# Attention and two MLPs on one NeuronCore: another order of issue, and block 0 transposed in full rows

## The chip, the core and the metric

The kernel runs on one NeuronCore of a Trainium2 chip. The engines are TensorE (PE; its weight loads are listed apart as PEld), VectorE (DVE), ScalarE (ACT), GpSimd (POOL) and SyncE (SP), which issues the DMAs. The metric is device time in microseconds, the median of the runs of one kernel.

## The reference, cut to what matters

```python
# x: (2, 4096, 192), weight_gen: (2, 4096, 8, 7); 8192 tokens in all
w = softmax(weight_gen, axis=-1)                     # 7 taps for each of 8 heads
x_pad = 6 zero rows ahead of each batch's x
attn[b, s, h, :] = sum_k w[b, s, h, k] * x_pad[b, s + k, h, :]     # 24 columns a head
h1 = attn.reshape(8192, 192) @ w1_in                 # 192 -> 2048
z  = (h1 * sigmoid(h1)) @ w1_out                     # 2048 -> 192
h2 = z @ w2_in                                       # 192 -> 2048
P  = a[0] + a[1]*h2 + a[2]*h2**2 + a[3]*h2**3
Q  = 1 + |b[0]|*|h2| + |b[1]|*h2**2
out = (P / (Q + 1e-6)) @ w2_out                      # 2048 -> 192
```

All is fp32. For PE each fp32 operand is split into a high part, rounded to PE's fp32r format, and a low part, the rest (g1h and g1l, g2h and g2l, xh and xl, and the weights wa, wb, wo), and products of the parts are summed.

## The kernel before, in words

The 8192 tokens are cut into 16 blocks of 512, numbered 0 to 15. For a block the kernel makes the attention (products of x with the softmax weights, 4 and 3 taps at a time, and their sums), transposes it, and runs it through both MLPs. Each MLP is cut into 8 units of 256 of its 2048 columns, and a unit's tile is 128 x 1024.

Since the 192 columns are 128 + 64, PE is used as two halves of 64 rows each, which work at the same time ("64*128" in the rows); a matmul of one half has 512 columns. What both write lies in one PSUM bank pair, and one half writes one side of it while the other half writes the other. Then the sides change, and to keep them apart a `nop` on SP (line 388) waits for both halves and releases both.

Work is given out in operations with a short name, a dot and the block, such as `l2.5`. The ones used below:

- `M`, `m`: products for 4 and 3 taps (line 728, POOL or DVE); `p`, `r`, `a`: their sums (lines 738, 742 and 748)
- `Z.0`, `X`: load the rows of x (line 690); `W0`, `W1`: 84 and 16 transposes whose results aren't used, at the start (lines 766 and 761)
- `T`, `TR`: the block's transposes in halves of 64 rows, one side and then the other (line 799); `XH`, `XL`: the split of the result into xh and xl
- `A`, `K`: a unit's first-layer matmuls into the bank h, one side and then the other (10 and 8; `B`, `Q` in the second MLP); `S`, `H`, `L`: silu, g1h and g1l (ACT, ACT, and DVE line 901)
- `C`, `E`, `I`, `F`: a unit's second-layer matmuls into acc0 (6, 4, 6, 4; `D`, `P`, `J`, `R` into acc1)
- `U`, `V`, `u`, `w`, `Y`, `N`, `G`, `g`: the rational function of the second MLP; on DVE `u` (line 948) and `w` (line 951) read h in PSUM and t in SBUF, `Y` (line 957) and `g` (line 968) read SBUF alone
- `h`, `l`: g2h (POOL line 453, ACT line 451 or DVE line 455) and g2l (line 978, DVE or POOL), both from SBUF

The order is written out by hand in `ORDER` (lines 39 to 266), a list of 3957 entries. In `name@n:s` the number n chooses the engine from those that the operation allows, and s the buffer or bank that it gets. A `^` in front of it loads an activation table. `Plan.run` (line 304) issues the entries one after the other. PE operations go to `Lanes`, which keeps a queue and a clock for each half and always issues for the half that is behind. A `|` in front of a PE entry is a bar: it moves the clock of the lagging half on by one turn (as long as one matmul of 512 columns), so that this half gets less work then. Other operations wait in the list `later` until the PE work that they need is issued. The planner costs nothing at run time; the list alone sets each engine's order.

Of the kernel before, what the change touches and what calls it, by code (L numbers as in the profile page):

```python
# [20 lines left out]
P = 128  # L21
J = 64
JB = 4
NB = J // JB
BT = JB * P
D = 192
DL = D - P
# [22 lines left out]
    q0O340:D q0O341 q0O3h@1 q0O3x L4.0:h q1B0a1 q1B0a0 cr q1B040:B q1B041 X.2 AW.2 |A6.0:A F5.0 K6.0 C5.0 E2.0 E1.0  # L50
    E3.0 S6.0 H6.0:r q1A0a0 A7.0:D L6.0:d q1B0h1 q1B0x1 q1A040:A q1B0h0 q1B0x0 a3.1 I3.0 F3.0 I4.0 K7.0 E6.0 E5.0
    C3.0 E4.0 C4.0 C6.0 T.1:B S7.0 q1A0a1 q1A041 H7.0:s q1O0l0:c q1O1l1:l q1O1l0:i L7.0:n ||||I6.0 TR.1 F7.0 I5.0
    F6.0 F4.0 I7.0 q1A1l0:m q1O0a1 q1O0a0 q1A0h q1O040:D q1O041 q1A1l1:r q1A0x q1O0h q1O2l0:c XH0.1:q q1O0x XL0.1:y
    m1.2:g M1.2:k M3.2:v m2.2:o p1.2@1 m0.2:w M2.2:p M0.2:t r1.2@1 m3.2:x p3.2@1 p2.2@1 r2.2@1 p0.2@1 r0.2@1 r3.2@1
# [10 lines left out]
    P2.0 u4.0 w4.0 U6.0:x ^^N3.0 h0.0@1:a T.2:C D1.0 TR.2 h5.0:v Y4.0 r0.3 u6.0 l5.0@1:r E6.1 C7.1 J0.0 J2.0 J1.0
    R1.0 XH0.2:m G3.0 XL0.2:n EC.1:f V6.0:y EM.1 g3.0 R5.0 A0.2:C Y6.0 N4.0 G4.0 N6.0 w6.0 EA.1 XH1.1:k G6.0 h3.0:p
    l3.0:o a0.3@1:e a2.3 XL1.1:s l0.0:u g6.0 g4.0 D0.0 K0.2 R2.0 B7.0:A D3.0 P5.0 Q7.0 B1.1:B J5.0 J3.0 ^S0.2 V7.0:q
    H0.2:a Q1.1 h6.0:h L0.2:r Y7.0 U7.0:g D5.0 P3.0 D6.0 P0.0 l6.0@1:v A3.2:C V1.1:p ^^N7.0 G7.0 U1.1:l u7.0 w7.0
    h4.0@2:x g7.0 R0.0 J6.0 B2.1:A R6.0 K3.2 J4.0 Q2.1 s3e l4.0@1:y h7.0:b l7.0@1:j M1.3:t u1.1 w1.1 s3t ^S3.2
# [343 lines left out]
def kernel(  # L413
# [13 lines left out]
    pe, act, dve, pool, sp = nc.tensor, nc.scalar, nc.vector, nc.gpsimd, nc.sync  # L427
# [249 lines left out]
    def attention(b):  # L677
# [96 lines left out]
        if b == 0:  # L774
            plan.op("W1", b, "PE", warm_h, rd=[at[0], ("ident", 0), (*tp, 0)], wr=[("h", 0, 0, 0, 0)])
# [339 lines left out]
```

## Time and profile before

| | us |
|---|---|
| median of 3 runs | 1260.79 |
| the runs | 1259.11, 1260.79, 1264.77 |
| the profiled execution's own time | 1258.52 |
| its span in the profile | 1256.7 |
| PE busy | 1193.0 (95%) |
| PE weight loads busy | 1020.4 (81%) |
| DVE busy | 1143.7 (91%) |
| ACT busy | 1041.0 (83%) |
| POOL busy | 509.4 (41%) |

Busy time is a mean over two stages, the first 100 us, in which data and weights come in, and the steady part after it. A busy PE is not PE at its peak, since matmuls overlap. The chain of waits is the sequence of work followed back from the last instruction, at each step to what released it.

### The profile page before, as it was taken

What the parts mean: (1) busy time and instruction counts of PE and PEld (TensorE: products, weight loads), DVE (VectorE), ACT (ScalarE), POOL (GpSimd) and SP (SyncE); (2) the same over time, 40 slices, a digit from 0 to 9 for tenths busy, and PEclk for the clock granted to TensorE, in tenths of its full rate; (3) what the DMA queues carried; (4) which work ended last, traced back from release to release, by engine and by line L of the source; (5) the groups of instructions that cost most, each with busy time, mean ns of one, the idle gap of its engine ahead of it and who ended that gap; (6) DMA issues with size and microseconds to landing.
All of it is one profiled execution on the core that took longest, in us unless ns stands there. A gap on an engine that the chain in (4) does not pass through costs nothing.

```text
span 1256.7 us, 24901 instructions
## 1 busy us (share of the span) xinstructions
PE 1193.0 (95%) x10340; PEld 1020.4 (81%) x10340; DVE 1143.7 (91%) x1037; ACT 1041.0 (83%) x1012; POOL 509.4 (41%) x326
## 2 busy tenths in 40 slices
PE   4989999999999999999999999999999999999997
PEld 4757778788788877899887888778888999789885
DVE  7989999899989888899999898998988989998997
ACT  4769988897898987798887788879897888789786
POOL 5874464345436333445214554332423313340332
PEclk9989999999999999999999999999999999999999
DMA  8650010102020010100100020010100001000001
GB/s 210 190 161 21 10 51 14 44 2 58 5 68 1 16 61 1 46 9 26 48 1 26 33 75 1 1 57 1 54 1 5 18 1 57 1 23 1 10 1 38
DMA packets 17753, 45.42 MB, mean 36 GB/s; under 512 B 2412, under 2 KB 9194, under 8 KB 17640
## 3 DMA queue, kind: packets, MB, share of 16 engines
q1 hardware_dynamic: 17640, 43.83, 11.6%
q8 instruction: 81, 1.33, 0.4%
q14 instruction: 32, 0.26, 0.1%
HBM read 31.73 MB, written 7.90 MB: 32 GB/s over the span
## 4 chain that ended last, share of the span: by engine, by line
PE 62%; DVE 19%; ACT 10%; issue 5%; SPq 2%; POOL 1%; DMA 1%; DVEq 0%; ACTq 0%; POOLq 0%
PE acc L786 31%; PE h L786 29%; DVE y L957 3%; DVE t L968 3%; DVE t L948 3%; DVE t L951 2%; DVE g1l L901 2%; ACT y L942 2%; ACT t L938 1%; DVE pr L728 1%; ACT y L962 1%; ACT h L893 1%; ACT g1h L897 1%; ACT y L965 1%; DVE dec L602 1%
## 5 line engine op out<-in xcount | busy, mean ns | idle before, releaser
L786 PE MATMUL h<-xh,wa 64*128 64x512 f32 x2048 | 464.6, 397 | 23.1 <-DVE t L951 9.1
L786 PEld LDWEIGHTS h<-xh,wa 64*128 64x128 f32 x2048 | 284.2, 185 | 76.5 <-SPq L388 17.2
L786 PE MATMUL h<-xl,wa 64*128 64x512 f32 x1024 | 312.8, 390 | 0.1
L786 PE MATMUL h<-xh,wb 64*128 64x512 f32 x1024 | 311.5, 389 | 0.0
L786 PE MATMUL acc<-g1h,wo 64*128 64x512 f32 x1536 | 299.0, 393 | 0.5 <-DVE t L951 0.4
L786 PE MATMUL acc<-g2h,wo 64*128 64x512 f32 x1536 | 292.6, 392 | 3.7 <-SPq L388 3.2
L978 POOL TENSOR_TENSOR g2l<-t,g2h 128x1024 fp32r<-128x1024 f32 x66 | 169.3, 2567 | 219.3 <-ACT g2h L451 62.5
L786 PEld LDWEIGHTS acc<-g2h,wo 64*128 64x128 f32 x1536 | 208.6, 184 | 27.5 <-SPq L388 6.9
L786 PEld LDWEIGHTS acc<-g1h,wo 64*128 64x128 f32 x1536 | 208.9, 185 | 24.5 <-SPq L388 3.8
L786 PE MATMUL acc<-g2l,wo 64*128 64x512 f32 x1024 | 213.7, 393 | 6.0 <-DVE g2l L978 4.1
L786 PE MATMUL acc<-g1l,wo 64*128 64x512 f32 x1024 | 212.4, 397 | 3.1 <-DVE g1l L901 2.6
L968 DVE SCALAR_TENSOR_TENSOR t<-t,a_sb,y 128x1024 f32<-128x1024 f32 x128 | 185.4, 1455 | 5.0 <-ACT y L965 4.0
L957 DVE SCALAR_TENSOR_TENSOR y<-y,b_sb 128x1024 f32<-128x1024 f32 x128 | 184.1, 1447 | 5.7 <-ACT y L942 5.4
L901 DVE TENSOR_TENSOR g1l<-h,g1h 128x1024 fp32r<-128x1024 f32 x128 | 155.5, 1219 | 35.3 <-ACT g1h L897 28.5
L728 POOL TENSOR_TENSOR pr<-xw,aw 128x768 f32<-128x768 f32 (+1 forms) x81 | 126.6, 1572 | 138.4 <-DVE t L968 41.4
L893 ACT ACTIVATE h<-h 128x1024 f32<-128x1024 f32 x128 | 129.2, 1012 | 60.6 <-PE h L786 59.8
L948 DVE TENSOR_TENSOR t<-t,h 128x1024 f32<-128x1024 f32 x128 | 155.5, 1215 | 23.5 <-ACT t L938 13.4
L786 PEld LDWEIGHTS h<-xl,wa 64*128 64x128 f32 x1024 | 164.2, 185 | 13.2 <-DVE xl L820 0.5
L938 ACT ACTIVATE t<-h,a_sb 128x1024 f32<-128x1024 f32 x128 | 153.8, 1203 | 24.9 <-PE h L786 15.8
L786 PEld LDWEIGHTS h<-xh,wb 64*128 64x128 f32 x1024 | 163.7, 185 | 12.6
L942 ACT ACTIVATE y<-h,b_sb 128x1024 f32<-128x1024 f32 x128 | 142.2, 1112 | 33.0 <-PE h L786 11.3
L951 DVE SCALAR_TENSOR_TENSOR t<-t,a_sb,h 128x1024 f32<-128x1024 f32 x128 | 163.6, 1279 | 4.8 <-ACT y L942 1.2
(78 smaller groups left out, 1859.0 us busy)
## 6 DMA issues: line engine op xcount, KB each, us to landing
xw<-in_x_dram SPq DMA_DIRECT2D x14, 960.0 KB, 5.5
raw<-in_moe_w_out_dram SPq DMA_DIRECT2D x16, 383.5 KB, 5.8
out_dram<-of SPq DMA_DIRECT2D x15, 384.0 KB, 2.8
e<-e SPq DMA_DIRECT2D x32, 128.0 KB, 2.3
raw<-in_moe_w_in_dram SPq DMA_DIRECT2D x16, 255.9 KB, 6.3
raw<-in_moe_w_in_dram SPq DMA_DIRECT2D x4, 511.8 KB, 4.5
aw<-wsm SPq DMA_DIRECT2D x14, 112.0 KB, 2.5
sm<-in_weight_gen_dram SPq DMA_DIRECT2D x3, 448.0 KB, 3.6
```

What stands on the lines that cost most here:

```text
L602: dve.scalar_tensor_tensor(out=view(i).bitcast(I32), in0=low, scalar=13, in1=st[tops][:, i, 0:n].bitcast(I32), op0=ALU.logical_shift_right ...
L728: e.tensor_tensor(out=p.rearrange("p k (h g) -> p k h g", g=G), in0=st[xw][:, j + k0:j + k0 + n, :].rearrange("p k (h g) -> p k h g", g=G) ...
L786: return pe.matmul(out=out, lhsT=w, rhs=x, start=start, stop=stop)
L893: act.activation(out=st[hb], in_=st[hb], func=AF.Silu)
L901: dve.tensor_tensor(out=t, in0=st[hb], in1=st[gh].bitcast(F32), op=ALU.subtract)
L938: act.activation(out=q, in_=st[hb], func=AF.Identity, scale=a_sb[:, 3:4], bias=a_sb[:, 2:3])
L942: act.activation(out=q, in_=st[hb], func=AF.Abs, scale=b_sb[:, 1:2])
L948: dve.tensor_tensor(out=st[t], in0=st[t], in1=flat(), op=ALU.mult)
L951: dve.scalar_tensor_tensor(out=st[t], in0=st[t], scalar=a_sb[:, 1:2], in1=flat(), op0=ALU.add, op1=ALU.mult)
L957: dve.scalar_tensor_tensor(out=st[y], in0=st[y], scalar=b_sb[:, 0:1], in1=st[y], op0=ALU.add, op1=ALU.mult)
L968: dve.scalar_tensor_tensor(out=st[t], in0=st[t], scalar=a_sb[:, 0:1], in1=st[y], op0=ALU.add, op1=ALU.mult)
L978: e.tensor_tensor(out=q, in0=st[t], in1=st[gh].bitcast(F32), op=ALU.subtract)
```

## The change

It has two parts. In `attention`, block 0 gets a new operation `WT`: 8 transposes over all 128 rows (function `rows`) in place of the 16 in halves of `T` and `TR`. All other blocks keep those.

```diff
+        def rows(e):
+            for a in range(2):
+                for j in range(JB):
+                    pe.transpose(
+                        out=st[tp][:, a, j * P:(j + 1) * P], in_=st[ao][:, j, a * DL:a * DL + P], identity=ident
+                    )
+
         at = [(*ao, j) for j in range(JB)]
...
-        first, second = turn(tp, ao)
-        plan.op("T", b, "PE", first, rd=[*at, ("ident", 0)], wr=[(*tp, 0)])
-        plan.op("TR", b, "PE", second, rd=[*at, ("ident", 0), (*tp, 0)], wr=[(*tp, 0)])
-        if b == 0:
+        if b:
+            first, second = turn(tp, ao)
+            plan.op("T", b, "PE", first, rd=[*at, ("ident", 0)], wr=[(*tp, 0)])
+            plan.op("TR", b, "PE", second, rd=[*at, ("ident", 0), (*tp, 0)], wr=[(*tp, 0)])
+        else:
+            plan.op("WT", b, "PE", rows, rd=[*at, ("ident", 0)], wr=[(*tp, 0)])
             plan.op("W1", b, "PE", warm_h, rd=[at[0], ("ident", 0), (*tp, 0)], wr=[("h", 0, 0, 0, 0)])
```

The other part is a new `ORDER`, 3956 entries in place of 3957, of which this is the first line before and after:

```diff
-    s0l X.0 s1l q0B0l0:u q0B0l1:w Z.0 q0A0l0:g q0A0l1:i s2l:o q0O0l0:h q0O1l1:t q0O0l1:m q0O1l0:v cl q0A1l0:r s0m cn
+    s0l cn X.0 s0m s0d ^^s0e s0t s0n@1 cz:f s2l:r s1l Z.0 M0.0@1:o q0A0l1:s M2.0@1:q q0B0l0:u M1.0@1:a s2m q0B0l1:g
```

It moves entries, gives 292 operations another engine, has 82 bars in place of 35 and 81 table loads in place of 85. Line numbers after line 766 rise by up to 9 (L786 becomes L795, L799 becomes L808, L901 L910, L948 L957, L951 L960, L957 L966, L968 L977, L978 L987).

At the start of PE, a piece of the difference (tp and h are PSUM banks, ident the identity matrix, ao the attention's output, xw rows of x):

```order
-L1110 UNCONDITIONAL_BRANCH
+L1119 UNCONDITIONAL_BRANCH
 L766 MATMUL tp<-ident,xw 128x128 x84
-L799 MATMUL tp<-ident,ao 128x64 x16
+L771 MATMUL tp<-ident,ao 128x128 x8
```

Between the 84 transposes of `W0` and the 16 of `W1` stood the 16 transposes in halves of `T.0` and `TR.0`; now the 8 of `WT.0` stand there.

On DVE around unit 2 of block 5 in the second MLP, near 502 us in the trace of before, there stands in a row before:

```order
L455 CAST g2h_5896<-t_5526 128x1024
L901 TENSOR_TENSOR g1l_5972<-h_5913,g1h_5961 128x1024
L978 TENSOR_TENSOR g2l_5974<-t_5526,g2h_5896 128x1024
L957 SCALAR_TENSOR_TENSOR y_5947<-y_5947,b_sb_69 128x1024
L901 TENSOR_TENSOR g1l_6018<-h_5950,g1h_6000 128x1024
L901 TENSOR_TENSOR g1l_6033<-h_5902,g1h_6013 128x1024
```

and after:

```order
L455 CAST g2h_5876<-t_5599 128x1024
L977 SCALAR_TENSOR_TENSOR t_5753<-t_5753,a_sb_68,y_5739 128x1024
L910 TENSOR_TENSOR g1l_5911<-h_5824,g1h_5874 128x1024
L957 TENSOR_TENSOR t_5913<-t_5913,h_5855 128x1024
L960 SCALAR_TENSOR_TENSOR t_5913<-t_5913,a_sb_68,h_5855 128x1024
L748 TENSOR_TENSOR ao_5948<-pr_5096 128x192
L748 TENSOR_TENSOR ao_5948<-pr_4997 128x192
L742 TENSOR_TENSOR pr_5292<-pr_5292 128x384
L966 SCALAR_TENSOR_TENSOR y_5898<-y_5898,b_sb_69 128x1024
```

The g2l of that unit (`l2.5`, L978 before) has left DVE for POOL, and instructions that read h in PSUM (L910, L957, L960) stand in its place.

On PE at unit 4 of block 6 in the first MLP, where the bank h passes from `A4.6` to `K4.6`, there stands in a row before:

```order
L786 MATMUL h_5794<-xl0_5219,wa00_71 128x512
L786 MATMUL acc1_5235<-g2h_5652,wo1_78 128x512
L786 MATMUL h_5794<-xl0_5219,wb0_75 128x512
L786 MATMUL acc1_5235<-g2h_5652,wo1_78 128x512 x5
L786 MATMUL h_5794<-xh0_5188,wa00_71 128x512 x2
L786 MATMUL h_5794<-xh0_5188,wa01_72 128x512 x2
```

and after:

```order
L795 MATMUL h_5824<-xh0_5188,wb0_75 128x512
L795 MATMUL acc0_5506<-g1l_5562,wo0_77 128x512
L795 MATMUL h_5824<-xl0_5234,wa00_71 128x512
L795 MATMUL h_5824<-xl0_5234,wb0_75 128x512
L795 MATMUL h_5824<-xh0_5188,wa00_71 128x512
L795 MATMUL h_5824<-xh0_5188,wa01_72 128x512
```

Five matmuls into acc1 stood between the two sides of that bank, and now none does.

## Rows read from the trace of the kernel before

**Rows 1.** The page: busy time, share of the span and instructions of each engine.

```profile
PE 1193.0 (95%) x10340; PEld 1020.4 (81%) x10340; DVE 1143.7 (91%) x1037; ACT 1041.0 (83%) x1012; POOL 509.4 (41%) x326
```

**Rows 2.** Windows: stretch, length, busy us of each engine, granted clock, DMA share, GB/s.

```profile
0.00:100.00 100.00, 76.27 (x568) 59.82 (x570) 83.88 (x103) 62.38 (x79) 66.30 (x61) 0.95 0.63 182
100.00:1240.00 1140.00, 1106.33 (x9689) 953.34 (x9686) 1052.11 (x926) 973.50 (x928) 440.67 (x264) 1.00 0.07 23
1240.00:1256.70 16.70, 10.44 (x89) 7.22 (x87) 7.69 (x10) 5.12 (x7) 2.41 (x1) 0.90 0.19 71
```

**Rows 3.** Timeline near 835 us, PE: start, us, what, [idle before <-releaser].

```profile
835.31 0.39 PE L786 MATMUL h<-xh,wb 64*128 64x512 f32 x1
...
835.54 0.39 PE L786 MATMUL h<-xl,wa 64*128 64x512 f32 x1
...
836.04 0.18 PEld L786 LDWEIGHTS acc<-g2h,wo 64*128 64x128 f32 x1 [0.54 <-SPq L388]
...
836.04 0.50 PE L786 MATMUL h<-xh,wa 64*128 64x512 f32 x1
```

**Rows 4.** The page: the chain that ended last, by engine and by line.

```profile
PE 62%; DVE 19%; ACT 10%; issue 5%; SPq 2%; POOL 1%; DMA 1%; DVEq 0%; ACTq 0%; POOLq 0%
```

**Rows 5.** Lines by form: busy us, mean ns of one, then idle before and releasers.

```profile
L786 PEld LDWEIGHTS h<-xh,wa 64*128 64x128 f32 x2048 | 284.2, 185 | 76.5 <-SPq L388 17.2 <-issue 13.0 <-DVE g1l L901 8.2
L968 DVE SCALAR_TENSOR_TENSOR t<-t,a_sb,y 128x1024 f32<-128x1024 f32 x128 | 185.4, 1455 | 5.0 <-ACT y L965 4.0
L957 DVE SCALAR_TENSOR_TENSOR y<-y,b_sb 128x1024 f32<-128x1024 f32 x128 | 184.1, 1447 | 5.7 <-ACT y L942 5.4
L951 DVE SCALAR_TENSOR_TENSOR t<-t,a_sb,h 128x1024 f32<-128x1024 f32 x128 | 163.6, 1279 | 4.8 <-ACT y L942 1.2
L901 DVE TENSOR_TENSOR g1l<-h,g1h 128x1024 fp32r<-128x1024 f32 x128 | 155.5, 1219 | 35.3 <-ACT g1h L897 28.5 <-issue 2.6 <-POOL ao L748 1.4
L978 DVE TENSOR_TENSOR g2l<-t,g2h 128x1024 fp32r<-128x1024 f32 x62 | 81.9, 1323 | 1.5 <-PE acc L786 1.0
```

**Rows 6.** Timeline at 502 us: a g2l on POOL and one on DVE.

```profile
502.39 2.39 POOL L978 TENSOR_TENSOR g2l<-t,g2h 128x1024 fp32r<-128x1024 f32 x1 [4.90 <-PE h L786]
502.40 3.46 DVE L978 TENSOR_TENSOR g2l<-t,g2h 128x1024 fp32r<-128x1024 f32 x1
```

**Rows 7.** The chain in order of time, DVE's two longest pieces: start, us, what.

```profile
1212.69 3.43 DVE t L968
1218.48 2.34 DVE t L968
```

**Rows 8.** Timeline of the start, around block 0's transposes.

```profile
13.15 11.59 PE L766 MATMUL tp<-ident,xw 128*128 128x128 f32 x84 [13.15 <-DMA xw<-in_x_dram]
...
24.67 0.81 PE L799 MATMUL tp<-ident,ao 64*128 64x64 f32 x8
24.81 3.02 SPq L690 DMA_DIRECT2D xw<-in_x_dram  x4
...
28.36 0.69 PE L799 MATMUL tp<-ident,ao 64*128 64x64 f32 x8 [2.89 <-SPq L388]
...
28.98 3.12 PE L761 MATMUL h<-ident,ao 128*128 128x128 f32 x16
...
30.22 1.23 DVE L820 TENSOR_TENSOR xl<-tp,xh 128x1024 fp32r<-128x1024 f32 x1
...
32.03 0.72 PE L786 MATMUL h<-xh,wa 64*128 64x512 f32 x4
```

**Rows 9.** Waits: who <- whom, total us, count, longest us.

```profile
PEld h L786 <- SPq L388: 17.2, 43, 1.1
PEld acc L786 <- SPq L388: 15.4, 41, 1.5
```

More of the change, by code (lines that the diff above doesn't have):

```diff
@@ L50 @@
[L50 to L54, printed above, removed]
@@ L65 @@
[L65 to L69, printed above, removed]
@@ new lines @@
+    q0B0x0 q0A0a1 p1.0@1 r1.0@1 q0B0h1 a2.0@1 r3.0@1 q0A040:C q0A041 a3.0 a1.0@1 q0A0h s2n@1 q0B0x1 WT.0 W1.0:B
+    XH0.0:w q0A0x XL0.0:y A0.0 K0.0 s2s q0O0a0 ca q0O0a1 q0O040:D q0O041 q0O1a0 A1.0:A q0O0h q0O140:C s1t q0O1a1
+    q0A1l1:n q0O0x s1n@1 K1.0 q1B0l1:m q0O141 ^S0.0 A2.0:D K2.0 q0O1h m3.1:p m1.1@1:q M1.1@1:b q0O2l1:s s3l:d H0.0:l
+    q0O2l0:g S1.0 H1.0:c q1A0l0:t q0A1a0 L0.0:o p1.1@1 q0A1a1 L1.0:i q0O3l0:a q0A140:A q0A141 q0O1x S2.0 M3.1:e
+    H2.0:v AW.2 A3.0:B K3.0 L2.0:k M0.1:q I0.0:C I1.0 q0O3l1:n I2.0 q1B0l0:r q0O2a1 q0A1h q0A1x F2.0 S3.0 M2.1@1:j
@@ new lines @@
+    J3.0 XH0.2:m Q7.0 h6.0@2:d N4.0 P1.0 XL0.2:n l6.0@1:q G4.0 EA.1 P3.0 D2.0 A0.2:C V7.0:j g4.0 U7.0:t J2.0 K0.2
+    Y7.0 XH1.1:k D3.0 N7.0 XL1.1:s D6.0 P6.0 G7.0 h4.0@2:v |B1.1:B a0.3@1:e u7.0 a2.3@1 J4.0 Q1.1 w7.0 ^S0.2 D4.0
+    H0.2:i g7.0 B2.1:A V1.1:u L0.2:w l4.0@1:j R6.0 U1.1:l Q2.1 A3.2:C u1.1 w1.1 U2.1:h p3.3@1 J6.0 h7.0@1:c K3.2
+    Y1.1 |A1.2:B S3.2 r3.3 P4.0 H3.2:f a3.3 K1.2 p1.3@1 V2.1:d L3.2:q R4.0 J7.0 S1.2 u2.1 l7.0@1:r |B3.1:C H1.2:v
+    w2.1 D7.0 Q3.1 L1.2:x M2.4:t B0.1:A U3.1:c r1.3@1 I3.2:B V3.1:j F0.2 a1.3 R7.0 u3.1 F1.2 M0.4:y P7.0 Q0.1 ^^N1.1
@@ new lines @@
+    H6.4:d E3.4 E4.4 S5.4 H5.4:b L6.4:u Q4.3 a1.6 h1.3:c I6.4 A7.4:A U4.3:x h2.3:g L5.4:n C6.4 V4.3:e l2.3@1:f E6.4
+    u4.3 w4.3 K7.4 B6.3:C S7.4 l1.3@1:k E5.4 H7.4:o T.5:D F6.4 L7.4:h TR.5 I5.4 XH0.5:r Q6.3 XL0.5:d F5.4 FT.2:A
+    I7.4 l3.3:v ^^N5.3 P2.3:D D0.3 V6.3:u Y4.3 D2.3 U6.3:j Y6.3 C7.4 R0.3 G5.3 J0.3 m0.7:o u6.3 N4.3 F7.4 P3.3
+    m1.7:q w6.3 FR.2 G4.3 R1.3 E7.4 g5.3 FE.2 D3.3 P1.3 N6.3 M0.7@1:n P0.3 C5.4 g4.3 G6.3 A1.5:C EC.4:p FA.2 R3.3
+    g6.3 J2.3 EM.4 R2.3 O.2 h4.3@1:k h5.3@1:l m2.7@1:h B7.3:A M1.7@1:b h6.3@1:v D4.3 l5.3:g K1.5 l6.3:u Q7.3 J3.3
@@ new lines @@
+    L7.7:i I7.7 XL0.8:g FT.5:A U6.6:c F7.7 F6.7 B7.6:B u6.6 E6.7 ^^N4.6 w6.6 C7.7 C6.7 Y5.6 V6.6:m E7.7 G4.6 FR.5
+    Y6.6 Q7.6 EC.7:l J3.6:C FE.5@1 V7.6:e EM.7 R1.6 R2.6 FA.5 U7.6:f J0.6 Y7.6 O.5 A0.8:A N5.6 g4.6 P0.6 N7.6 D0.6
+    u7.6 K0.8 G7.6 EA.7 D3.6 N6.6 w7.6 D1.6 P2.6 G5.6 g7.6 A1.8:B XH1.7:u h4.6@2:o R0.6 h7.6:e G6.6 R3.6 XL1.7:l
+    J4.6 l7.6:r B2.7:D ^S0.8 P1.6 K1.8 H0.8:j g6.6 h6.6@2:f P3.6 S1.8 L0.8:m Q2.7 H1.8:a J1.6 g5.6 B0.7:A U2.7:t
+    h5.6@2:y l4.6@1:w P7.6 D2.6 V2.7:i L1.8:p Q0.7 u2.7 A3.8:B V0.7:s l6.6@1:k w2.7 R4.6 U0.7:q R7.6 J5.6 u0.7 K3.8
@@ new lines @@
+    Q6.8 L6.9:h h3.8:a H7.9:k C6.9 r2.11@1 L7.9:g U6.8:i E6.9 T.10:C h0.8:e C7.9 V6.8:r E7.9 l3.8@1:m B7.8:A
+    h1.8@1:j u6.8 F7.9 I7.9 F6.9 w6.8 ^^N5.8 l0.8:d R2.8:B J0.8 EC.9:k J3.8 l1.8:p G5.8 EM.9 R3.8 R0.8 X.12 N4.8
+    g5.8 R1.8 TR.10 Q7.8 G4.8 Y6.8 D3.8 EA.9 P2.8 D2.8 XH1.9:y P0.8 V7.8:o U7.8:t g4.8 a2.11@1 h4.8:k XL1.9:g D1.8
+    P1.8 l4.8@1:f ||B2.9:D N6.8 u7.8 D0.8 G6.8 Q2.9 w7.8 XH0.10:h J1.8 Y7.8 B0.9:A XL0.10:v U2.9:s V2.9:a J2.8 Q0.9
+    N7.8 A1.10:C h5.8@2:j g6.8 G7.8 u2.9 P4.8 l5.8@1:n D4.8 U0.9:r w2.9 D5.8 h6.8@1:p P3.8 K1.10 u0.9 A0.10:D w0.9
@@ new lines @@
+    EC.11:p XL0.12:d D2.10 FE.9 EM.11 G4.10 a1.13@1 l3.10:a D1.10 D0.10 P0.10 N6.10 P1.10 FA.9 h5.10:f A1.12:C O.9
+    N7.10 r2.13@1 EA.11 A2.12:D l5.10:v XH1.11:g M3.13:e J3.10 G7.10 XL1.11:r K1.12 G6.10 a2.13@1 R3.10 m3.13@1:l
+    K2.12 g4.10 X.14 J2.10 ^S1.12 R5.10 p3.13 A0.12:A H1.12:n g6.10 S2.12 D5.10 h6.10:p L1.12:k K0.12 H2.12:b J5.10
+    l6.10:w S0.12 B2.11:C g7.10 h4.10@1:l R6.10 J6.10 H0.12:i L2.12:t l4.10@1:x Q2.11 L0.12:h B3.11:D V2.11:s
+    h7.10@2:f D6.10 U2.11:c l7.10@1:m Q3.11 u2.11 R4.10 V3.11:q B0.11:A r3.13@1 w2.11 U3.11:p P7.10 Q0.11 Y3.11
@@ new lines @@
+    S7.13 F4.13 Q4.12 r2.14 H7.13:a l3.12:d C6.13 V4.12:u L7.13:p B6.12:B E6.13 l2.12:b B7.12:A ^^G0.12 a2.14@1
+    Y4.12 I4.13 U4.12:l Q7.12 g0.12 N1.12 E7.13 E5.13 u4.12 h0.12:c C5.13 G1.12 E4.13 Q6.12 w4.12 l0.12@1:i U7.12:v
+    I6.13 N5.12 u7.12 F7.13 U6.12:r g1.12 I7.13 D2.12:D V7.12:s F5.13 u6.12 J0.12 h1.12:j N4.12 C4.13 w7.12 P0.12
+    V6.12:f l1.12@1:h D1.12 I5.13 G5.12 w6.12 T.14:A G4.12 R0.12 Y6.12 TR.14 C7.13 XH0.14:e R1.12 Y7.12 J3.12
+    EC.13:a N6.12 R3.12 EM.13 XL0.14:y R2.12 X.15 J1.12 N7.12 AW.15 g4.12 A1.14:B G6.12 D3.12 G7.12 EA.13 P3.12
```

407 lines of the change are left out of this document (191 added, 216 removed).

## The prediction, made before the changed kernel ran

> **What bounds the kernel now.** The busy shares come first: PE 95%, DVE 91%, ACT 83%, POOL 41% [rows 1]. Then the windows: from 100 to 1240 us PE is busy 1106 of 1140 us and DVE 1052, at a granted clock of 1.00; in the first 100 us it is 76 of 100 [rows 2]. So there are two stages with different limits, a start that waits for data and a long steady part in which PE is nearly full and DVE close behind.
>
> How full PE is, the turns tell. Two 64-row halves of PE work side by side, and within a half matmuls of 512 columns start 0.23 us apart (835.31, 835.54) [rows 3]; over the steady part the spacing is 0.227. A unit of either MLP has 38 such matmuls, 19 turns of the pair of halves, so 16 blocks x 2 x 8 units x 19 = 4864 turns, and 4864 x 0.227 = 1104 us, 88% of the span. No order of issue takes that away. What an order can win is the rest, 1256.7 - 1104 = 153 us: the start, times in which one half stands, and times in which both stand. Read by halves, the trace has both at work 1088 us, one alone 61 us and none 104 us; of these 104 us, 36 lie in the first 100 us. The chain of waits says whose those are: PE 62%, DVE 19%, ACT 10%, issue 5%, SP's queue 2% [rows 4]. The order can gain through DVE and ACT, and lose through PE's own steps.
>
> A Trainium skill page would read PE's room otherwise; that is a rival below.
>
> **What is on DVE's part of the chain.** Among DVE's 1024-element instructions those that read one operand from PSUM take 1279 (L951) and 1219 ns (L901), and those with both operands in SBUF take 1455 (L968) and 1447 ns (L957) on average [rows 5]. The difference is not the operation, since L951 and L968 do the same one: it is POOL. At 502.39 us POOL begins a g2l, DVE begins its own g2l 0.01 us later and takes 3.46 us [rows 6] where such a one takes 1.32 [rows 5]: 2.14 us more, nearly all of POOL's 2.39. Instructions that read PSUM don't stretch with POOL beside them. I call this a meeting at the port. Its bill on DVE: L968 128 x (1455 - 1279) = 22.5 us, L957 128 x (1447 - 1279) = 21.5, g2l 62 x (1323 - 1219) = 6.4; the products, the g2h casts and the weight decoding, worked out alike, some 34 to 39; together 84 to 90 us. Laid over the chain of waits piece by piece (252 DVE pieces, 250.8 us; the two longest are L968 at 1212.69 with 3.43 and at 1218.48 with 2.34 [rows 7]), 44.6 us of that excess lie on the chain. The rest is hidden in DVE's slack.
>
> **The change part by part.**
>
> *Block 0's transposes.* T.0 and TR.0 (16 in 64-row halves) go, WT.0 (8 in full rows) comes. From 24.67 to the end of TR.0 at 28.36 + 0.69 = 29.05 are 4.38 us, of which 2.89 is idle behind SP: the `nop` that parts the two sides stands on SP's queue behind four DMA issues of 3.02 us [rows 8]. WT.0 has no sides and no `nop`. A full 128-row transpose costs 11.59 / 84 = 0.138 us in W0 [rows 8], so 8 cost 1.1. Gain 4.38 - 1.1 = 3.3 us, if nothing else is late. Next is XL0.0 (DVE, 1.23 us), which now ends at 31.45, 0.6 us ahead of A0.0 at 32.03 [rows 8]; it too starts when its transposes end, so it moves with them. The new list also issues block 0's own x rows ahead of the weight loads, and W0 waits 13.15 us for exactly such a load [rows 8]; against that, later weight loads can become late in a stage where DMA holds 63% of its time [rows 2]. I take -4, bounds -6 and 0 (0 if the weights decide the start).
>
> *Meetings at the port.* The list moves 292 operations to another engine. POOL has 300 operations instead of 315 (fewer products, six g2h fewer, g2l 66 to 65), DVE some 4 us more work, ACT 15 more operations and 4 activation-table loads fewer. In the lists, 81 of POOL's 315 entries are followed on DVE by an entry with two SBUF operands, now 60 of 300, from 26% to 20%. At the unit shown for DVE, the old list puts a g2l on DVE behind the one on POOL, the collision of 502.39; the new one puts L910, L957 and L960 there (its own line numbers, before's L901, L948 and L951), which read PSUM, and the g2l goes to POOL. Price: POOL entries that begin as a meeting cost DVE 78.9 us at 105 of 315, the others 5.7; a quarter fewer in rate, times 15 entries fewer, is about 30% off. 44.6 x 0.30 = 13 us on the chain. Bounds: 0 (meetings happen as engines come free, not as the list is written: POOL begins 1.5 us ahead of its place in the median) and -30 (two thirds of 44.6). I take -13.
>
> *PE's own steps.* The bars (turns by which one half may lag) rise from 35 in all to 82, and the new list changes the side of a bank without a matmul of another in between 97 times, where the old did 19 times. Such a change is a round trip from PE over SP to PE. At 835.54 the last matmul of one side starts, the next at 836.04 [rows 3]: 0.50 us instead of 0.23, so 0.27 lost. That is the price of steady ones; the mean over all of the old list's, most at the start or the end, is 0.39. With two matmuls in between it costs 0.05, with four none. Besides, two matmuls of the same half in a row (the other standing) rise by 108, worth half a turn each where nothing fills it. At full price: 78 x 0.27 = 21, 108 x 0.227 / 2 = 12, in all +33. The other half mostly has work at these places (on the chain such waits are just 17.2 and 15.4 us of PE's weight loads for 84 waits [rows 9]), and part of these turns replace idle time that is there anyway: both halves are at work only 1088 of the 1257 us. I take a quarter, +8; bounds 0 and +33 (the dearer price for the first term gives +42, which I leave as the tail).
>
> *The rest at nothing.* ACT's 15 operations more are covered by its 17% of idle time and the 4 table loads less; DVE's 4 us lie in its 88 us of idle time in the steady part, but cost up to 4 if the meetings stay.
>
> **The sum.** The profiled execution's own time is 1258.52, its span 1256.7. 1258.5 - 4 - 13 + 8 = 1249.5. The median of the runs, 1260.79, is 2.3 above it: 1251.
>
> **The rivals.**
>
> *The port doesn't change (1265).* That the change doesn't do what it says. For: what decides a meeting is which DVE instruction stands behind the one that releases POOL, and there the share with two SBUF operands is 51% in the old list and 53% in the new. POOL is idle 59% of the time [rows 1], so it starts when released. Then -4 + 0 + 8: 1258.5 + 4 + 2.3 = 1265. Against: the worst collisions (3.43 to 3.46 us) are of the kind the new list parts.
>
> *Side changes paid in full (1277, slower).* Place: PE's steady part, where it is 97% busy [rows 2]. At full price +33 - 4 - 13 = +16: 1258.5 + 16 + 2.3 = 1277. It decides from 17 of the 33 us on, where the sum is zero. For: PE has little room for turns lost. Against: a half that waits leaves the array to the other one, and the wait rows of SP's `nop` are short, 0.4 us each [rows 9].
>
> *The meetings fall by two thirds (1227).* The new list parts most of them, and the steps are covered: 1258.5 - 4 - 30 + 0 + 2.3 = 1227. For: DVE is second on the chain with 19% [rows 4]. Against: POOL still does 300 operations on the same port.
>
> *PE has room (1244).* PE's weight loads are busy 81%, its matmuls 95% [rows 1]. If the 81% were the measure, lost turns would fall into room and cost nothing: 1258.5 - 4 - 13 + 0 + 2.3 = 1244. Against: one weight load takes 185 ns [rows 5] of a turn of 227, so a PE with no gap at all would show 82%. The Trainium skill, "Perfetto Trace Analysis", section "Identifying the Most-Contended Engine", says that matmul busy time is no good measure for TensorE and that the share of LDWEIGHTS is; by that DVE (91%) would be the bound here and PE not. This trace doesn't bear it out, as 185 of 227 ns shows.
>
> **How the numbers follow.** The forecast, 1251, has a chance of 0.42; its own range is 1243 to 1259, from the bounds of startup and steps around the port term. Port unchanged 0.20, steps in full 0.14, two thirds 0.14, room in PE 0.10. A measurement of this kernel tells about 0.5% (6.3 us) from no change, so the same is 1254.5 to 1267.1. Faster: 0.31 of the forecast's 0.42, and 0.14 and 0.10: 0.55. Same: 0.11 of the forecast, 0.17 of the unchanged port: 0.28. Slower: 0.14 and 0.03: 0.17. For 8 in 10 the range takes the forecast, the unchanged port and the room in PE whole, and about half of each end: 1230 to 1272.
>
> **What the profile after would show.** Startup: WT.0 about 1.1 us, no idle behind SP there, first A0.0 near 28 us. Port: the means of L977 (was L968) and L966 (was L957) fall from 1455 and 1447 towards 1400, and DVE's share of the chain from 19% to 18%; if they stay, the first rival. Steps: PE's weight loads' waits for SP's `nop` grow from 84 and 32.6 us; under 10 us more is the forecast, over 17 the second rival. ACT's table loads are 4 fewer. Wrong altogether if a stage starves: weight loads that come late in the first 100 us, or gaps of PE over 2 us behind ACT, whose queue got longer.

## The result, and the profile after

The changed kernel takes 1275.97 us in the median (four runs, 1274.64 to 1276.78), the kernel before 1259.95 beside it: a ratio of 1.0122, with an interval of 1.0088 to 1.0157. It is slower by 16 us where I forecast some 10 us faster. The time lies above the range (1230 to 1272) and 1 us from the rival in which the side changes are paid in full (1277).

The page of after, engines and then the chain of waits (for before [rows 1, 4]):

```profile
PE 1223.8 (96%) x10332; PEld 1013.4 (80%) x10332; DVE 1096.0 (86%) x1037; ACT 1047.5 (82%) x1023; POOL 470.0 (37%) x311
...
PE 75%; ACT 8%; DVE 6%; issue 2%; SPq 1%; DMA 0%; POOL 0%; DVEq 0%; ACTq 0%
```

PE does the same matmuls but for the 8 transposes saved, and yet is busy for 31 us more, while its weight loads fell from 81% to 80%: what was added is not work. The Trainium skill, "Perfetto Trace Analysis", section "Identifying the Most-Contended Engine", says that matmul busy time is not a good measure of how near TensorE is to its limit, and names the weight loads' busy share among those to use instead. The trace agrees on the first, since the busy share rose in a kernel that got slower. DVE lost 48 us of busy time and went from 19% to 6% of the chain. By these rows the port part came out larger than I had it, and PE took more than all of it.

Lines by form, after (busy us, mean ns of one | idle before, releasers). L977 and L966 are the L968 and L957 of [rows 5], L960 and L987 its L951 and L978:

```profile
L977 DVE SCALAR_TENSOR_TENSOR t<-t,a_sb,y 128x1024 f32<-128x1024 f32 x128 | 166.7, 1312 | 12.8 <-ACT y L974 11.5
L966 DVE SCALAR_TENSOR_TENSOR y<-y,b_sb 128x1024 f32<-128x1024 f32 x128 | 168.8, 1325 | 11.0 <-ACT y L951 10.8
L960 DVE SCALAR_TENSOR_TENSOR t<-t,a_sb,h 128x1024 f32<-128x1024 f32 x128 | 163.5, 1279 | 6.5 <-ACT y L951 3.3
L987 DVE TENSOR_TENSOR g2l<-t,g2h 128x1024 fp32r<-128x1024 f32 x63 | 76.8, 1231 | 4.3 <-PE acc L795 2.0 <-POOL g2h L453 1.4 <-PE h L795 0.3
```

The forms with both operands in SBUF fell from 1455 and 1447 ns to 1312 and 1325, close to the 1279 of the form that reads PSUM, which has not moved. The two together are (143 + 122) ns x 128 = 34 us shorter.

Waits after (who <- whom: total us, times, longest us), against [rows 9]:

```profile
PEld h L795 <- SPq L388: 39.6, 86, 1.6
...
PEld acc L795 <- SPq L388: 32.6, 73, 1.4
```

Waits of PE for SP's `nop` went from 32.6 us in 84 to 72.2 us in 159. One of them stands at the place where the bank h passes from `A4.6` to `K4.6`, the third piece of order shown with the change. PE there, in the timeline (start, us, what):

```profile
502.98 0.39 PE L795 MATMUL acc<-g1l,wo 64*128 64x512 f32 x1
502.99 0.39 PE L795 MATMUL h<-xl,wb 64*128 64x512 f32 x1
503.47 0.50 PE L795 MATMUL h<-xh,wa 64*128 64x512 f32 x1
503.48 0.49 PE L795 MATMUL acc<-g1l,wo 64*128 64x512 f32 x1
503.81 0.39 PE L795 MATMUL h<-xh,wa 64*128 64x512 f32 x1
```

Both halves start at 502.98 and both next at 503.47: 0.49 us instead of 0.23. The half that works on acc needs nothing from the `nop`. Its matmul stands behind the waiting one in PE's instruction stream and starts 0.01 us after it. So it is at the other places: by the order of issue, at none of the 97 changes with no matmul in between does a matmul issued behind the waiting one start before it, and at 9 in 10 of them the other half goes on within 0.05 us of it. This is what I had not priced: a side change with nothing in between stops both halves.

The rows of matmuls, read by halves, up to PE's last matmul:

| | both at work | one alone | none |
|---|---|---|---|
| before | 1087.7 us | 60.6 | 103.6 |
| after | 1066.8 | 91.8 | 109.9 |
| after without bars (first experiment) | 1088.6 | 59.8 | 84.0 |

### The profile page after: what moved, and what is told of

Read it like the earlier page. It is cut to its first block, busy times and chain, and to the rows that moved or that the text cites. A ratio compares the mean times of both kernels' runs of the same rounds, so it can differ in the third digit from the quotient of the medians.

```text
span 1273.4 us, 24930 instructions
## 1 busy us (share of the span) xinstructions
PE 1223.8 (96%) x10332; PEld 1013.4 (80%) x10332; DVE 1096.0 (86%) x1037; ACT 1047.5 (82%) x1023; POOL 470.0 (37%) x311
## 4 chain that ended last, share of the span: by engine, by line
PE 75%; ACT 8%; DVE 6%; issue 2%; SPq 1%; DMA 0%; POOL 0%; DVEq 0%; ACTq 0%
PE acc L795 38%; PE h L795 35%; DVE t L960 1%; ACT t L947 1%; ACT y L971 1%; ACT y L951 1%; DVE t L957 1%; ACT y L974 1%; PE to L1015 1%; PE tp L808 1%; ACT h L902 1%; ACT g1h L906 1%; DVE g1l L910 1%; SPq L928 1%; DVE t L977 1%
## 5 line engine op out<-in xcount | busy, mean ns | idle before, releaser
L795 PE MATMUL h<-xh,wa 64*128 64x512 f32 x2048 | 508.6, 401 | 13.2 <-DVE t L960 2.9
L795 PEld LDWEIGHTS h<-xh,wa 64*128 64x128 f32 x2048 | 303.1, 185 | 79.3 <-SPq L388 39.6
L795 PE MATMUL h<-xl,wa 64*128 64x512 f32 x1024 | 337.7, 390 | 0.1
L795 PE MATMUL h<-xh,wb 64*128 64x512 f32 x1024 | 336.2, 390 | 0.0
L795 PE MATMUL acc<-g1h,wo 64*128 64x512 f32 x1536 | 329.8, 397 | 4.9 <-DVE wo L623 1.8
L795 PE MATMUL acc<-g2h,wo 64*128 64x512 f32 x1536 | 311.3, 393 | 2.4 <-SPq L388 0.6
L795 PEld LDWEIGHTS acc<-g1h,wo 64*128 64x128 f32 x1536 | 224.3, 185 | 36.7 <-SPq L388 13.5
L987 POOL TENSOR_TENSOR g2l<-t,g2h 128x1024 fp32r<-128x1024 f32 x65 | 170.5, 2626 | 212.0 <-DVE g2h L455 98.0
L795 PEld LDWEIGHTS acc<-g2h,wo 64*128 64x128 f32 x1536 | 216.9, 184 | 31.0 <-SPq L388 11.4
L795 PE MATMUL acc<-g1l,wo 64*128 64x512 f32 x1024 | 239.9, 397 | 1.6 <-DVE g1l L910 0.7
L795 PE MATMUL acc<-g2l,wo 64*128 64x512 f32 x1024 | 236.4, 394 | 1.0 <-DVE t L960 0.3
L910 DVE TENSOR_TENSOR g1l<-h,g1h 128x1024 fp32r<-128x1024 f32 x128 | 155.6, 1220 | 62.6 <-ACT g1h L906 50.7
L957 DVE TENSOR_TENSOR t<-t,h 128x1024 f32<-128x1024 f32 x128 | 155.6, 1216 | 37.8 <-ACT y L951 19.9
L795 PEld LDWEIGHTS h<-xl,wa 64*128 64x128 f32 x1024 | 173.6, 185 | 14.7 <-DVE xl L829 0.8
L795 PEld LDWEIGHTS h<-xh,wb 64*128 64x128 f32 x1024 | 172.8, 185 | 14.1
L966 DVE SCALAR_TENSOR_TENSOR y<-y,b_sb 128x1024 f32<-128x1024 f32 x128 | 168.8, 1325 | 11.0 <-ACT y L951 10.8
L977 DVE SCALAR_TENSOR_TENSOR t<-t,a_sb,y 128x1024 f32<-128x1024 f32 x128 | 166.7, 1312 | 12.8 <-ACT y L974 11.5
L795 PE MATMUL h<-xl,wb 64*128 64x512 f32 x512 | 169.3, 389 | 0.0
L960 DVE SCALAR_TENSOR_TENSOR t<-t,a_sb,h 128x1024 f32<-128x1024 f32 x128 | 163.5, 1279 | 6.5 <-ACT y L951 3.3
```

Source lines behind the costliest of these rows:

```text
L795: return pe.matmul(out=out, lhsT=w, rhs=x, start=start, stop=stop)
L910: dve.tensor_tensor(out=t, in0=st[hb], in1=st[gh].bitcast(F32), op=ALU.subtract)
L957: dve.tensor_tensor(out=st[t], in0=st[t], in1=flat(), op=ALU.mult)
L960: dve.scalar_tensor_tensor(out=st[t], in0=st[t], scalar=a_sb[:, 1:2], in1=flat(), op0=ALU.add, op1=ALU.mult)
L966: dve.scalar_tensor_tensor(out=st[y], in0=st[y], scalar=b_sb[:, 0:1], in1=st[y], op0=ALU.add, op1=ALU.mult)
L977: dve.scalar_tensor_tensor(out=st[t], in0=st[t], scalar=a_sb[:, 0:1], in1=st[y], op0=ALU.add, op1=ALU.mult)
```

## The experiments

**1. The list after without its bars.**

```diff
-    V7.4:n X.9 Y6.4 |||A2.6:B h5.4@1:l l3.4:x ... u7.4 w7.4 ^S2.6 p3.8 |||A1.6:A
+    V7.4:n X.9 Y6.4 A2.6:B h5.4@1:l l3.4:x ... u7.4 w7.4 ^S2.6 p3.8 A1.6:A
```

and so for all 82.

> The kernel after with all 82 bars taken out of its list and nothing else; every other engine keeps its order, only which half of TensorE is served next changes. Side changes of a bank with no matmul in between fall from 97 to 45, those with at most two from 163 to 99. Theory A (the side changes are paid in full): 52 x 0.27 us less, or up to 52 x 0.5 with both halves standing, so 14 to 26 us off 1276: 1250 to 1262, and the waits of the weight loads for SP fall from 80 us to some 50. Theory B (the new list lost its time in the start and in data that come late, and the bars only fill times in which TensorE would stand anyway): within 5 us of 1276.

Measured: 1239.01 us, a ratio to before of 0.9818 (0.9800 to 0.9836). The bars cost 37 us, more than theory A said, and without them the new list is faster than the old one by 21. The page and the waits:

```profile
PE 1196.5 (97%) x10332; PEld 1015.6 (82%) x10332; DVE 1097.8 (89%) x1037; ACT 1046.6 (85%) x1023; POOL 471.3 (38%) x311
...
PE 76%; ACT 9%; DVE 5%; issue 2%; SPq 1%; POOL 1%; DMA 0%; DVEq 0%; ACTq 0%; POOLq 0%
```

```profile
PEld h L795 <- SPq L388: 23.4, 53, 2.0
PEld acc L795 <- SPq L388: 19.2, 45, 1.4
```

The waits for SP fall from 72.2 to 42.6 us, and PE is busy for 27 us less with the same 10332 matmuls. The port's part stays: DVE is 5% of the chain. Of the 37 us the changes with no matmul in between account for some 23: in the same half, the time beyond one turn at these places sums to 42.0 us over 97 in the kernel after (0.43 each) and to 18.6 over 45 here; before it was 9.2 over 19. (The rows don't name a matmul's half. These sums rest on how the matmuls are told apart by the order of issue; other ways of doing it put 15 to 26 us in place of the 23.) I had 0.27 for the steady ones. That holds where both halves end together (median here 0.27); where one ends half a turn earlier, it is 0.44 (median of after).

**2. WT.0 alone in the kernel before.**

```diff
-... X.1 s2d@1 s1n@1 T.0 TR.0 XH0.0:w ...
+... X.1 s2d@1 s1n@1 WT.0 XH0.0:w ...
```

> The kernel before with one part of the change alone: WT.0 in place of T.0 and TR.0. Theory A: the 2.89 us behind SP and the half transposes go, the first matmul of layer 1 moves from 32.0 to about 28.8 us, and 0 to 3 us of it are left at the end: 1257 to 1260. Theory B (the start is set by the weights or the sums of the attention): the first matmul stays at 32 us and the time at 1260.

Measured: 1260.51, ratio 0.9997 (0.9980 to 1.0014). The idle time behind SP is gone and layer 1 begins 2.94 us sooner than in [rows 8], after a wait of 1.03 us for xh. It then waits twice more:

```profile
26.13 1.94 PE L761 MATMUL h<-ident,ao 128*128 128x128 f32 x16 [0.15 <-DVE wb L623]
...
29.09 0.50 PE L795 MATMUL h<-xh,wa 64*128 64x512 f32 x2 [1.03 <-ACT xh L825]
...
30.35 0.54 PE L795 MATMUL h<-xh,wa 64*128 64x512 f32 x2 [0.76 <-DVE wa L623]
...
31.48 0.80 PE L795 MATMUL h<-xl,wa 64*128 64x512 f32 x2 [0.16 <-DVE xl L829]
...
32.80 0.79 PE L795 MATMUL h<-xh,wa 64*128 64x512 f32 x2
```

DVE splits weights (L623) in the time gained, and XL0.0 still begins at 30.22. When the second side begins (32.80, in the kernel before 33.55) 0.75 us of the 3 are left, and at the end none: theory A for the first matmul, theory B for the time.

**3 and 4. GpSimd's low parts as a fill with zeros, in both kernels.**

```diff
-            e.tensor_tensor(out=q, in0=st[t], in1=st[gh].bitcast(F32), op=ALU.subtract)
+            if e is pool:
+                e.memset(q.bitcast(F32), 0.0)
+            else:
+                e.tensor_tensor(out=q, in0=st[t], in1=st[gh].bitcast(F32), op=ALU.subtract)
```

> The kernel before, in which GpSimd's 66 low parts g2l are replaced by a fill with zeros (the output lacks these low parts): GpSimd reads nothing there and holds the port for under half as long. Theory A (the port is on this kernel's path, 44.6 us of it): 10 to 25 us faster, 1235 to 1250. Theory C (what the port costs VectorE is hidden behind TensorE anyway): within 4 us of 1260.

> The same edit in the kernel after (65 low parts, and the output lacks them). Here only 4.1 us of VectorE's excess lie on the chain of waits. Theory A and theory C alike: within 4 us of 1276. If it falls by 10 us or more, the port still is on the path of the new list and the trace was misread.

Measured: before falls to 1229.08 (ratio 0.9743, 0.9723 to 0.9764), by 31 us; after stays, at 1276.59. Lines by form of the former:

```profile
L957 DVE SCALAR_TENSOR_TENSOR y<-y,b_sb 128x1024 f32<-128x1024 f32 x128 | 175.7, 1382 | 5.7 <-ACT y L942 5.5
L968 DVE SCALAR_TENSOR_TENSOR t<-t,a_sb,y 128x1024 f32<-128x1024 f32 x128 | 170.7, 1340 | 6.7 <-ACT y L965 5.8
...
L979 POOL MEMSET g2l<- 128x1024 f32 x66 | 63.2, 963 | 183.9 <-PE acc L786 87.6 <-PE h L786 31.9 <-DVE t L968 17.0
```

66 instructions of 2567 ns became such of 963, and DVE's two forms fell from 1447 and 1455 to 1382 and 1340. So the meetings with POOL's g2l were on the path of the kernel before, by up to 31 us, more than theory A's 25 (the g2l also come sooner, which this edit doesn't keep apart). In the kernel after the same edit changes nothing.

**5. The bars of the list after, in the list before.** The bars of before go, those of after stand on the operations of the same name:

```diff
-    q1O140:A q1O141 q1O1h@1 q1O1x q1A1a0 ||||||A2.1:D E7.0 K2.1 ... ||A1.1:A K1.1
+    q1O140:A q1O141 q1O1h@1 q1O1x q1A1a0 ||||A2.1:D |||||E7.0 ||K2.1 ... A1.1:A K1.1
```

> The opposite of the first experiment: the kernel before with its own list, engines and table loads, but the 82 bars of the list after on the operations of the same name in place of its own 35. Side changes with no matmul in between rise from 19 to 90. Theory A (bars push the sides of a bank together, and each such change is paid): 71 x 0.27 to 71 x 0.5, so 19 to 36 us slower, 1279 to 1296. Theory D (the loss needs the rest of the new list; in this one TensorE waits for VectorE often enough to hide it): within 8 us of 1260.

Measured: 1297.04, ratio 1.0275 (1.0252 to 1.0299): 36 us slower, just above the upper end of theory A. The waits for SP double here too, in a kernel that has all else from before:

```profile
PEld h L783 <- SPq L385: 36.2, 77, 1.9
PEld acc L783 <- SPq L385: 28.7, 64, 1.4
```

(L385 is the `nop` in this file.) The time beyond one turn at changes with nothing in between sums to 44.9 us over 90. DVE remains 16% of the chain, so PE still waits for it often, and the loss is there all the same: theory D falls.

**6 and 7. Bars kept and operations exchanged; no bars and operations exchanged.** The sixth list has 40 exchanges. For instance, the PE operations in a row:

```diff
-K0.0 A1.0 ... K3.0 I0.0 ... F5.0 E4.0
+A1.0 K0.0 ... I0.0 K3.0 ... E4.0 F5.0
```

> The kernel after with all its 82 bars kept, but 46 exchanges of neighbouring TensorE operations (none moved by more than one place in TensorE's own order), so that side changes with no matmul in between fall from 97 to 32 and those with at most two from 163 to 74. Theory A (the price is the side change, the bars only bring it about): 65 x 0.43 = 28 us off 1276, so 1243 to 1255. Theory E (the price is the half that the bars leave empty): 1268 to 1276.

> The kernel after without bars and with 22 such exchanges (none by more than three places): 24 side changes with no matmul in between instead of 45, 60 with at most two instead of 99. Theory A: 21 x 0.4 = 8 us at most off 1239, so 1231 to 1237. Theory E: 1239.

Measured: 1258.31 (0.9971, 0.9956 to 0.9986) with bars, 18 us better than after and not the 28 expected; 1248.07 (0.9885, 0.9863 to 0.9908) without bars, 9 us worse than the first experiment, which neither theory had. Both did to the side changes what they should: the time beyond one turn at changes with nothing in between fell from 42.0 to 15.3 and from 18.6 to 11.0 us. What they gave back stands in the waits. In the seventh:

```profile
PEld acc L791 <- ACT tops L585: 5.6, 1, 5.6
PEld h L791 <- DVE g1l L906: 5.4, 9, 2.1
PE acc L791 <- DVE wo L619: 5.2, 1, 5.2
PEld h L791 <- DVE xl L825: 5.2, 8, 1.9
```

All waits of PE and its loads for DVE and ACT together are 41 us in the first experiment and 80 in the seventh. As I read it, an exchange that puts `A` ahead of its neighbour asks for xl, or a free bank, sooner, and one that puts `K` later delays the silu behind it. Theory E is not borne out as the whole of it, since the sixth keeps all 82 bars and gains 18 us.

**8. The list before without its bars.**

> The kernel before without its 35 bars: 12 side changes with no matmul in between instead of 19. Theory A: 7 x 0.27 = 2 us less, 1256 to 1261; what the lists differ in beside bars is then worth some 20 us, which the port pays. Theory E: some 10 us less.

Measured: 1257.97, ratio 0.9980 (0.9962 to 0.9998). The 35 bars of before cost 2.7 us, as theory A said. With the first experiment this gives what the rest of the change is worth, WT.0 included: 1239.01 - 1257.97 = -19.0 us.

**9. Five exchanges with slack, and four bars.** The list of the first experiment with five exchanges, `F1.2` behind `P7.0` for one, and with four bars put back at the start and the end:

```diff
-... R7.0 u3.1 F1.2 M0.4:y P7.0 Q0.1 ...
+... R7.0 u3.1 M0.4:y P7.0 F1.2 Q0.1 ...
```

> The kernel after without its bars, with five exchanges of neighbouring TensorE operations alone: only second-layer operations are put later, and only operations whose inputs stood ready at least 0.5 us before in the trace are put earlier (P6.11 behind B7.11, F1.2 behind P7.0, I3.9 behind Q4.8, F5.1 behind R5.0, I3.0 behind E3.0), and four bars at the start and the end (one on K7.0, one on C0.0, two on FT.15). Side changes with no matmul in between: 33 instead of 45. Theory A: 12 x 0.27 = 3 us or a little more off 1239, so 1234 to 1238; the waits of TensorE for VectorE and ScalarE stay at some 41 us, unlike in the exchange of 22, which raised them by 38. If order has no more to give: 1239.

Measured: 1232.60, ratio to before 0.9781 (0.9748 to 0.9815), 6 us better than the first experiment and the fastest of all with the whole computation. Its waits for SP and its page:

```profile
PEld h L791 <- SPq L384: 17.9, 42, 2.7
...
PEld acc L791 <- SPq L384: 16.9, 38, 1.7
```

(L384 is the `nop` in this file.)

```profile
PE 1189.8 (97%) x10332; PEld 1052.2 (86%) x10332; DVE 1096.6 (89%) x1037; ACT 1046.3 (85%) x1023; POOL 469.6 (38%) x311
```

The waits for DVE and ACT did not grow (40 us). At the changes with nothing in between the time beyond one turn fell from 18.6 to 17.1 us alone, so these don't account for the 6 us. This run changes two things, the exchanges and the four bars; where the rest comes from I did not settle.

**10 and 11. Three more nops a side change.**

```diff
+                for _ in range(3):
+                    step = self.sp.nop()
```

> The kernel after in which each side change is made longer by three further nops on SP (17 ns each in the records, with what lies between them some 0.05 to 0.15 us together). Theory A: the 97 changes with no matmul in between and the 66 with two pay nearly all of it, 163 x 0.05 to 163 x 0.15: 8 to 24 us slower, and at least one and a half times what the kernel before pays for the same. A theory in which side changes lie beside other waits: under 4 us.

> The same edit in the kernel before, where 19 side changes have no matmul in between and 64 have two: 83 x 0.05 to 83 x 0.15 at most, so 2 to 12 us slower, about half of what the kernel after pays.

Measured: 1275.76 and 1259.65, as without them. This tells nothing: the traces have 670 and 680 of these instructions, as many as the kernels after and before, so the additional ones are not in the program that ran.

**12. GpSimd's low parts as a fill, without bars** (the edit of 3 in the kernel of 1).

> The kernel after without bars, in which GpSimd's 65 low parts g2l are replaced by a fill with zeros (the output lacks them). The kernel before gained 31 us by this and the kernel after nothing. If the new list has taken the port off the path for good (5.9 us of VectorE's excess on the chain): within 5 us of 1239. If the bars alone hid the port's cost in the kernel after: 10 us or more faster.

Measured: 1240.53, where the first experiment has 1239.01. The bars did not hide what POOL's g2l cost. The new list has taken that off the path.

**13 to 15. The side change lengthened for good.** Four instructions on SP, each waiting for the one before:

```diff
-                step = self.sp.nop()
-                for i in was[1].values():
-                    self.tc.add_manual_dep(step.ins, i.ins.name, self.after, reason="row groups of a bank")
+                for _ in range(4):
+                    back, step = step, self.sp.nop(nofuse=True)
+                    for i in was[1].values() if back is None else (back,):
+                        self.tc.add_manual_dep(step.ins, i.ins.name, self.after, reason="row groups of a bank")
```

> The kernel after, in which each side change goes through four instructions on SP in place of one, each waiting for the signal of the one before (the plain nops of the experiment before last were merged away: its trace has 670 of them, as the kernel after). Call d the time that this adds to a change; the trace gives it, as the growth of the gap at changes with no matmul in between. Theory A: nearly all of the 97 changes with none and the 66 with two in between pay d, so 140 d to 200 d is added to 1276 (14 to 20 us at d = 0.1). Theory E (the loss lies in halves left empty, the change itself is mostly hidden): under 50 d.

> The same edit in the kernel before (19 changes with none and 64 with two in between). Theory A: 50 d to 110 d added to 1260, about half of what the kernel after pays (5 to 11 us at d = 0.1). Theory E: under 50 d in both.

> The same edit in the kernel after without bars (45 changes with none and 54 with two in between). Theory A: 80 d to 130 d added to 1239, so the distance to the kernel after, 37 us, grows with d by some 60 d. Theory E: the distance stays at 37 us.

Measured: 1324.55, 1286.71 and 1274.11 us. The gap at changes with two matmuls in between grows from 0.04 to 0.26, 0.04 to 0.23 and 0.04 to 0.24 us, and at those with none from 0.44 to 0.68, 0.36 to 0.55 and 0.27 to 0.49 (medians), so d is about 0.22. The kernel after pays 48.6 us (221 d), the kernel before 24.0 (109 d, beside 1262.72 in the same comparison), the one without bars 35.1 (160 d). The kernel before is between 1259.95 and 1262.72 us in the comparisons from which these come, so they are good to some 3 us. The distance between with and without bars grows from 37 to 50 us, by 61 d, where theory A said some 60. The kernel after pays twice what before does. That after and the one without bars pay more than theory A's 200 d and 130 d is partly from changes with four in between, whose mean gap rises from 0.02 to 0.07 as well. In the kernel after the loads wait thus (L389 is the line of all four):

```profile
PEld h L796 <- SPq L389: 69.3, 130, 1.8
PEld acc L796 <- SPq L389: 60.2, 116, 1.3
```

Had the wait been hidden, to lengthen it by 0.22 us would have cost little. It is paid at once.

## Why the prediction was wrong, point by point

**The step that failed** is "I take a quarter, +8": I took three quarters of the side changes' price as overlapped by the other half. Measured, the bars of after against those of before cost 37.0 - 2.7 = +34 us, the whole of the full price of +33 that gave the second rival, 1277. The reason that I gave for the quarter, that the other half has work at these places, is true, and useless: its next matmul stands behind the waiting one (503.47 and 503.48). Nor does a half that waits leave the array to the other one, as I had against that rival.

That 34 lies beside 33 is luck in part. The +33 priced 78 more changes with nothing in between at 0.27 us, 21 us in all. The traces have 42.0 - 9.2 = 32.8 us for them, but the bars bring only 52 of them (97 against 45 in the first experiment); the others are in the new order itself.

The Trainium skill has the rule that I needed: "TensorE: Matmul & The Clock Gate", section "Step-by-step: what each phase is for", says that weight loads may be pulled ahead of matmuls, but matmuls stay in program order. The trace agrees at the waiting matmul, with 0.49 us between starts in both halves where 0.23 is usual. It differs beside it: of the two matmuls of `K4.6` that the piece of order shows in a row, the second starts at 503.81, and the one into acc that is issued behind both has started at 503.48. So the matmul that waited for the `nop` was passed by none, but another one was passed by one of the other half.

The rows on which I leaned, 84 waits of 0.4 us, showed short waits, and I took short for covered. They were few because the old list has only 19 such places, most in the start and at the end, and 64 with two matmuls in between. The price of one, 0.27, was also low; it is 0.43 on the mean in the kernel after.

How the 37 us split is settled in part. Some 23 us are the changes with nothing in between, 2.5 those with two (6.1 against 3.6). The other 11 or so lie elsewhere: the time with one half alone falls by 32 us when the bars go, worth half of that, and it overlaps with what the changes cause. No run kept the empty halves apart from the changes.

**The port.** Forecast -13 on the chain, with means towards 1400 ns. The means are 1312 and 1325, and of the 44.6 us of excess on the chain 4.1 are left. Of the 256 instructions in these two lines 80 ran beside POOL before and 50 after, and those that did were on average 0.24 us (L966) and 0.48 us (L977) shorter than before. So the count of neighbours in the lists (26% to 20%) understated it, and the count that spoke for the first rival (51% and 53%) misled: which instruction meets which is settled at run time. The third experiment puts the worth of POOL's g2l in the old list at up to 31 us, and the fourth and twelfth at nothing in the new one. No run changed the meetings alone within the new list.

**The start.** Forecast -4, measured 0 up to layer 1: the first matmul of layer 1 starts at 32.15 in after, at 32.03 before. In the timeline of after:

```profile
8.59 10.72 PE L766 MATMUL tp<-ident,xw 128*128 128x128 f32 x84 [8.59 <-DMA xw<-in_x_dram]
...
21.55 0.43 PE L771 MATMUL tp<-ident,ao 128*128 128x128 f32 x1 [2.24 <-POOL ao L748]
...
24.03 2.09 DVE L602 SCALAR_TENSOR_TENSOR dec<-raw,tops 128x512 int32<-128x512 int32 x2
...
26.03 1.14 DVE L748 TENSOR_TENSOR ao<-pr 128x192 f32<-128x192 f32 x1
...
27.23 1.78 PE L771 MATMUL tp<-ident,ao 128*128 128x128 f32 x7 [5.25 <-DVE ao L748]
```

The rows of x came 4.56 us sooner, as I said, and the wait behind SP is gone. The attention's last sums (L748) now stand behind the weight decoding on DVE and come at 26 to 27 us. I had written "if nothing else is late" and looked at XL0.0 alone. Half of the failure is also in the second experiment: without that delay the weights are next.

By 100 us the start has even lost. The windows after the start of layer 1, before and then after (stretch, length, busy us of each engine, granted clock, DMA share, GB/s):

```profile
32.00:100.00 68.00, 60.45 (x453) 44.66 (x454) 59.19 (x68) 49.17 (x61) 50.04 (x38) 0.95 0.55 171
33.00:100.00 67.00, 58.84 (x411) 43.49 (x409) 56.07 (x72) 46.31 (x58) 41.20 (x34) 0.92 0.54 173
```

By 100 us the old list has begun 436 matmuls of 512 columns, the new one 399, and 393 without bars. At two in 0.227 us this puts the new list 4 to 5 us behind, by estimate. Most of it falls between 40 and 50 us, where it begins 41 against 71: PE waits 1.79 us there for weights that DVE splits (L623), and after it, from 47 to 49 us, its granted clock is 0.51, the lower of the two levels (1.2 GHz). It comes near one of the signs that I had set, weights that are late in the first 100 us.

**The sum of the parts that were right by luck or by reason.** Port and start together: forecast -17, measured -19.0 (first against eighth experiment). That these are so near is luck in part. The -19.0 is all that the new list does without its bars: it holds the 4 to 5 us lost by 100 us, and 45 changes with nothing in between where the eighth has 12. What is left must have given more than 19, and that it is the port is argued from the chain (19% to 5%), not shown by a run of its own. Added up as written, the forecast is 1249.5 + 2.3 = 1251.8, so 1252 and not 1251; nothing hangs on that.

The direction of the whole was decided by one term, for which the prediction named the condition: "it decides from 17 of the 33 us on". All were paid.

**What the signs said.** The sign that I set for the second rival, waits of PE for SP that grow by over 17 us, came: 39.6. The forecast's sign for the port (DVE's share of the chain 18%) was passed by far, 6%. ACT's longer queue did no harm: PE has no gap over 2 us behind ACT in the steady part. The rival with room in PE falls with the time, but my reckoning against it, that a PE with no gap would show 82% of weight loads, falls too: the ninth kernel shows 86%.

## What to carry to other kernels

Ask of a short wait who stands behind it in the same instruction stream. Here two halves of an engine are fed from one stream, a wait of one was a wait of both, and its price went by its length times its count, however much work the other half had.

When a new order is slower, separate its parts before giving it up. Here the order was good (-19 us) and the marks on it bad (+37 us). Lengthen a wait that you suspect and see whether the time grows with its count; look in the trace that it has grown first.

## What the runs showed of the hardware that was not expected

A side change through SP costs a PE with nothing in between 0.27 us when its halves end together and 0.43 us on average; with two matmuls in between 0.04, with four 0.02 on average. Three more dependent instructions on SP add 0.22 us, some 0.07 each, while each is recorded with 17 ns. Of two halves fed from one stream, a matmul of one half started 0.33 us ahead of one of the other half that is issued before it (503.48 and 503.81), while at 97 places none passed one that waited for the `nop`. A busy share of PE of 96% held 37 us that taking out the bars gave back.
